# An attention, mixture-of-experts and feed-forward kernel: weights' fetches issued by another engine, one more stored table, smaller conditional blocks

## The chip, the cores and the metric

The kernel runs as one program on one core of a Trainium2 chip. The metric is the device time of one execution in microseconds (us), from the first to the last instruction and a little around them; lower is better. The engines are named as the profile names them: PE (matmul; PEld is its load of weights), DVE (vector), ACT (activation), POOL (GpSimd) and SP (which only issues transfers). A trailing q (ACTq, SPq) is an engine's sequencer: branches, register loads, semaphores and the issue of transfers.

## The reference

```python
def reference(**kw):                      # float32 but for moe2's weights (float64)
    a = exp(phi - max); a /= sum          # attention over 32 memory slots
    attn = softmax(q @ (a^T k)^T / 8) @ (a^T v)
    x = attn as (4608, 512)
    # top-1 mixture of 8 experts, FE = 1024
    e = argmax(cosine(x, emb) / tau); gate = softmax(...)[e]
    x = gate * (relu(x @ w1[e]) @ w2[e])
    # feed-forward, FF = 2048
    h = x @ w_in
    return (h * sigmoid(1.702 * h)) @ w_out
```

The tokens are 4608 rows of 512. Each matrix product is made of three f16 products of high and low parts, so that it has f32 accuracy.

## The kernel before

The span has four stretches. **Attention** takes the first 240 us. During it tokens are sorted by expert into a DRAM table `xbuf`. From about 240 to 304 us four **early slots** (s = -4 to -1) run for the tokens of one expert `e0` that are known early. Then come the **slots** s = 0 to 31: each takes 128 sorted tokens of one expert through both layers. From slot 28 (683 us) a slot also does halves of the **feed-forward**, which runs alone from about 800 us to the end.

One slot of the loop (`slot`, L1108) issues, in an order set by the table TIMES: the first layer of slot s (`product`, L981, 96 matmuls of 128x128), its ReLU in two halves (`relu`: ACT L994, DVE L997), the second layer of slot s - 1 (`second`, L1006, 24 matmuls of 128x512), the store of slot s - 2 (`leave`), the making of x16 and its transposing load xT for slot s + 2 (`take`: ACT L962, DVE L967, SP L969), the gather of slot s + 5 (`gather`, POOL L952), and shares of the decoding of the feed-forward's weights. These arrive as float64 (tiles `raw`, 512 KB each, SP L1252, three buffers, and three more that `Weights.widen` opens just ahead of slot 0) and are turned into f32 by ACT (L1278), DVE (L1281 to L1295) and POOL (L1299, L1304). A piece's POOL step frees its buffer and issues the next load.

An expert's weights are four pieces of w1 and four of w2 (tiles `wr`, 512 KB each) in one set of buffers. When a slot begins a new expert, conditional blocks run (`when`: an If on a register that SP, and the other engines, load from the table `tabs`, L834): `change(0, s + 1)` and `change(1, s)`. A change takes the scale, splits the f32 pieces `wr` into f16 pieces `wh` (ACT L80 writes the high part, DVE L91 the low part, piece by piece), and then `further` fetches the next expert's pieces into the same buffers (L842, on SP): a fetch has to wait for L91 of its piece. Two more blocks per slot, `bound(0)` and `bound(1)`, take squares of the fetched pieces on ACT (L846). All these Ifs stand in the code of L1120, and all five engines run each of them. `early` fetches the second expert's eight pieces in the early slots (`further(k, 0)`).

Completions of SP's transfers are counted by a ring of a few semaphores, and a transfer waits for the one that had its semaphore before. In the branch of a change that is not taken, SP has to wait for the four semaphores that the fetches would have used and count them on itself. So SP meets an earlier fetch that has not landed at its next change block.

`leave` (L1034) has POOL copy the tokens' indices into the last columns of the tile y16 (L1039), DVE write the scale next to them (L1040), ACT and DVE write the two f16 halves (L1043, L1046), and SP store the tile to `yb` (L1048) and the scale to `ys` (L1049). `Ffn.load` reads index and scale back from `yb`.

Of the kernel before, what the change touches and what calls it, by code (L numbers as in the profile page):

```python
# [27 lines left out]
XW = 514  # L28
YI, YS, YW = 2 * DM, 2 * DM + 2, 2 * DM + 4
HEAD = 8  # L30
EARLY = 4
ALWAYS = NT // P - EARLY
MORE = 6
ALONE = 28
LAG = 1
FIRST = 22.9, 5.4, 14.39, 33.37, 36.61, 2.87
# [612 lines left out]
class Dispatch:  # L649
# [43 lines left out]
    def slots(self):  # L693
# [5 lines left out]
        def up():  # L699
            o.ni = s.tile([P, E], I32, tag="ni", name="ni")  # L700
            v.tensor_scalar(o.ni, g.cnt, float(P - 1), None, ALU.add)
# [20 lines left out]
        def sum2():  # L722
            self.end = s.tile([P, E], F32, tag="end", name="end")
            v.tensor_reduce(out=self.end, in_=o.t8, axis=AX.X, op=ALU.add)
# [9 lines left out]
        def pick2():  # L734
            o.sl = s.tile([PB, ncols], F32, tag="sl", name="sl")
            v.tensor_reduce(out=o.sl, in_=o.t, axis=AX.X, op=ALU.add)
# [48 lines left out]


WHY = "counts of tokens, bounded by their number"

# [7 lines left out]
class Moe:  # L796
# [3 lines left out]
    def __init__(self, g, w):  # L800
        self.g = g

        shapes = [4, FE // 4], [2, DM]
        self.wh = [[w.tile([P, 2, *shapes[k]], F16, name=f"wh{k}{i}") for i in range(4)] for k in range(2)]
        self.raws = [[w.tile([P, *shapes[k]], F32, name=f"wr{k}{i}") for i in range(4)] for k in range(2)]
        self.sc = w.tile([P, 2], F32, name="scw")

        self.scp = w.tile([P, 1], F32, name="scp")
        g.junk = self.junk = w.tile([P, 1024], BF16, name="wjunk")
        self.m = w.tile([P, 2, 4], F32, name="wm")  # L810

# [5 lines left out]
        self.regs = {}  # L817

    def buf(self, kind):
        g = self.g  # L820
        if kind == "xg":
            return g.xp.tile([P, XW], F32, tag="xg", name="xg", bufs=3)
        if kind == "x16":
            return g.xp.tile([P, 2 * DM], F16, tag="x16", name="x16", bufs=2)
        if kind == "xT":
            return g.xp.tile([P, 8, P], F16, tag="xT", name="xT", bufs=2)
        if kind == "hT":
            return g.mp.tile([P, 2, 8, P], F16, tag="hT", name="hT")
        return g.mp.tile([P, YW], F16, tag="y16", name="y16")

    def reg(self, k, s):

        if (k, s) not in self.regs:
            self.regs[k, s] = self.g.nc.values_load(self.g.tabs[0:1, k, s:s + 1] if s >= 0 else self.g.before0[:, s + EARLY:s + EARLY + 1],  # L834
                                                    engines=(mybir.EngineType.SP,) if k in (0, 3, 4) else mybir.ALL_ENGINES,
                                                    min_val=0, max_val=(E - 1, 1, self.g.ns, 1, NT)[k],
                                                    skip_runtime_bounds_check_because=WHY)
        return self.regs[k, s]

    def fetch(self, k, i, ev):  # L840
        w = (self.g.w1, self.g.w2)[k][bass.ds(ev, 1)].rearrange("o (k p) f -> p (o k) f", p=P)
        self.g.nc.sync.dma_start(out=self.raws[k][i], in_=w[:, 2 * i:2 * i + 2] if k else w[:, :, FE // 4 * i:FE // 4 * (i + 1)])  # L842

# [36 lines left out]
    def first(self):  # L880
# [55 lines left out]
    def when(self, s):  # L936
# [3 lines left out]
        return self.g.tc.If(self.reg(1, s) > 0)  # L940

    def index(self, s):

# [10 lines left out]
    def take(self, s):  # L954
# [4 lines left out]
        def high():  # L959
            o.x16 = self.buf("x16")  # L960
            o.f = o.xg[:, DM + 1:DM + 2]
            nc.scalar.activation(out=o.x16[:, 0:DM], in_=o.xg[:, 0:DM], func=AF.Copy, scale=o.f)  # L962
            o.c = g.small.tile([P, 1], F32, tag="pc", name="pc", bufs=5)
            nc.scalar.activation(out=o.c, in_=o.xg[:, DM:DM + 1], func=AF.Copy)
# [43 lines left out]
    def measure(self, s):  # L1008
# [3 lines left out]
        def square():  # L1012
            o.m = g.small.tile([P, 1], F32, tag="ym", name="ym")
            nc.scalar.activation(out=self.junk[:, 0:DM], in_=o.yp, func=AF.Square, accum_out=o.m)  # L1014

            o.fac = g.small.tile([P, 1], F32, tag="fac", name="fac", bufs=4)
            nc.scalar.activation(out=o.fac, in_=o.c, func=AF.Copy, scale=self.scp)
# [14 lines left out]
    def leave(self, s):  # L1032
# [77 lines left out]
    def slot(self, s, share, ffn):  # L1110
# [16 lines left out]

        def bound(k):
            return lambda: self.bound(k)

        add(0, [lambda a=a, fi=fi: self.product(s, a, fi) for a in range(2) for fi in range(4)], h)
# [8 lines left out]
        if s:  # L1140
# [15 lines left out]
        if s + 5 < end:  # L1156
            add(TG, [lambda: self.gather(s + 5)])
        add(0.2, share, 10.2 / max(len(share), 1))
        for _, _, f in sorted(ev, key=lambda e: e[:2]):
            f()  # L1160

    def run(self, ffn):
# [11 lines left out]
        self.layer2(s)  # L1174
        with self.when(s):
            self.bound(0)
            self.bound(1)
        with self.when(s - 1):
            self.bound(1)

# [19 lines left out]
    def bounds(self, s):  # L1200
        with self.when(s):
            for k in range(2):
                self.bound(k)

# [192 lines left out]
class Ffn:  # L1397
# [16 lines left out]
    def load(self, t):  # L1414
# [8 lines left out]
        nc.sync.dma_start(out=o.s, in_=g.ys[rows].rearrange("(o r) w -> o (r w)", o=1).to_broadcast([P, 2 * P]))  # L1423
        o.i = g.small.tile([P, 2, YW - YI], F16, tag="x2i", name="x2i")
        nc.sync.dma_start(out=o.i, in_=g.yb[rows, YI:].rearrange("(j p) w -> p j w", p=P))
        o.f = g.small.tile([P, 2], F32, tag="x2f", name="x2f")
# [37 lines left out]
    def layer2(self, t, j):  # L1464
        g, nc, o = self.g, self.g.nc, self.x[t]
        if j == 0:
            nc.vector.tensor_scalar(o.f, o.i.bitcast(F32)[:, :, (YS - YI) // 2], self.k[:, 1:2], None, ALU.mult)
# [7 lines left out]
        nc.scalar.activation(out=y, in_=op, func=AF.Copy, scale=o.f[:, j:j + 1])  # L1475
        nc.gpsimd.indirect_dma_start(out=g.out, out_offset=bass.IndirectOffsetOnAxis(ap=o.i.bitcast(I32)[:, j, 0:1], axis=0), in_=y, in_offset=None,  # L1476
                                     bounds_check=NT - 1, oob_is_err=False)
# [40 lines left out]
def tile_kernel(ctx, tc, q, k, v, phi, emb, tau, w1, w2, w_in, w_out, out):  # L1518
# [11 lines left out]

    g.yb = dram.tile([NT + P, YW], F16, name="yb")
    g.ys = dram.tile([NT + P, 1], F32, name="ys")
# [12 lines left out]
    with tc.manual_schedule():  # L1545
# [17 lines left out]
        at.close()  # L1563
        g.weights.widen(wsr.enter_context(tc.tile_pool(name="wsr", bufs=1, side="right", reuse_waits="tile")))

# [38 lines left out]
```

## Time and profile before

| | us |
|---|---|
| median of 3 runs (1527.42 to 1529.71) | 1528.2 |
| profiled execution, its own time | 1527.33 |
| its span | 1525.6 |
| TensorE's mean granted clock | 0.956 of full speed |

The span runs from the first to the last instruction; the profiled execution's own time is 1.7 us more. Rows give a start and a duration in us of the span; in a timeline, the brackets hold the engine's idle time before a row and what ended it.

### The profile page before, as it was taken

The page shows a single profiled execution, that of the slowest core. Times are in us where ns is not written, and L with a number is a line of the kernel's source. Part 1 is how long each engine was busy: PE and PEld are TensorE (multiplying, and loading weights), DVE is VectorE, ACT ScalarE, POOL GpSimd, SP SyncE. Part 2 cuts the span into 40 slices and gives each one's busy share as a digit, 9 for nine tenths or more (in the row PEclk, how much of TensorE's full clock was granted, in tenths as well). Part 3 has the DMA queues.
Part 4 walks back from the last instruction along what each step waited for, and adds up shares of the span by engine and source line. Part 5 has one row for each costly group of instructions (what it writes and reads, how often), then busy time and mean ns, then how long its engine had stood idle before and what let it go on. Part 6 is the DMA issues. An engine that isn't in the chain of part 4 may idle for free. (4 is left out here: it accounts for less than half of the span.)

```text
span 1525.6 us, 31172 instructions
## 1 busy us (share of the span) xinstructions
PE 1379.8 (90%) x11628; PEld 972.9 (64%) x11628; DVE 839.3 (55%) x2066; ACT 691.9 (45%) x1623; POOL 274.6 (18%) x269
## 2 busy tenths in 40 slices
PE   5979888978789789889999999999989999999997
PEld 4767666656557566667657556666646666666664
DVE  3887896887557755856335144443324444443332
ACT  3767774445545554756334134333313333333332
POOL 2543430453323333210100000000000000000000
PEclk9997678989999999999999999999999999999999
DMA  9999933699987996673213411110211111101100
GB/s 221 239 240 266 233 73 110 179 170 162 159 109 121 172 117 83 163 93 39 56 47 32 60 32 40 31 31 19 34 32 27 32 27 30 32 19 28 32 15 14
DMA packets 171628, 138.11 MB, mean 91 GB/s; under 512 B 104730, under 2 KB 152218, under 8 KB 171426
## 3 DMA queue, kind: packets, MB, share of 16 engines
q1 hardware_dynamic: 165186, 115.13, 41.0%
q0 software_dynamic: 6240, 20.50, 5.5%
q8 instruction: 101, 1.65, 0.5%
q14 instruction: 101, 0.83, 0.4%
HBM read 84.77 MB, written 30.38 MB: 75 GB/s over the span
## 5 line engine op out<-in xcount | busy, mean ns | idle before, releaser
L1472 PE MATMUL op<-wo,gt 128*128 128x512 f16 x1728 | 378.9, 381 | 20.8 <-DVEq L1503 10.1
L1438 PE MATMUL hp<-x2T,wi 128*128 128x256 f16 x3456 | 380.7, 273 | 5.4 <-DMA x2T<-yb 2.9
L1438 PEld LDWEIGHTS <-wi 128*128 128x128 f16 x3456 | 337.8, 98 | 48.9 <-issue 3.6
L1442 DVE TENSOR_TENSOR th<-hp,x2s 128x256 f32<-128x256 f32 x288 | 122.1, 424 | 386.9 <-PE hp L1438 383.3
L1472 PEld LDWEIGHTS <-gt 128*128 128x128 f16 x1728 | 169.5, 98 | 224.7 <-issue 17.9
L981 PE MATMUL hp<-xT,wh 128*128 128x128 f16 x3552 | 216.7, 224 | 33.7 <-ACTq L1120 12.6
L981 PEld LDWEIGHTS <-wh 128*128 128x128 f16 x3552 | 210.1, 101 | 48.5 <-issue 30.2
L1006 PE MATMUL yp<-wh,hT 128*128 128x512 f16 x888 | 204.0, 387 | 22.7 <-ACT wjunk L846 5.2
L1443 ACT ACTIVATE th<-th,fk 128x256 f32<-128x256 f32 x288 | 146.2, 508 | 166.2 <-DVE th L1442 163.7
L1475 ACT ACTIVATE o<-op,x2f 128x512 f32<-128x512 f32 x36 | 24.7, 687 | 342.2 <-PE op L1472 342.2
L1006 PEld LDWEIGHTS <-hT 128*128 128x128 f16 x888 | 86.2, 99 | 127.8 <-PEq L1120 16.1
L1476 POOL DMA_INDIRECT out_dram<-o,x2i x36 | 35.2, 977 | 709.9 <-ACT o L1475 653.6
L1462 DVE SCALAR_TENSOR_TENSOR gt<-th,gt 128x256 f16<-128x256 f32 x288 | 120.4, 418 | 2.6
L1452 DVE SCALAR_TENSOR_TENSOR th<-th,hp 128x256 f32<-128x256 f32 x288 | 118.2, 410 | 3.1 <-ACT th L1443 3.1
L1454 ACT ACTIVATE gt<-th 128x256 f16<-128x256 f32 x288 | 115.6, 401 | 3.3 <-DVE th L1452 3.2
L952 POOL DMA_INDIRECT xg<-xbuf,idx x38 | 43.0, 1131 | 181.9 <-ACTq L1120 42.4
L997 DVE SCALAR_TENSOR_TENSOR hT<-hp,hT 128x512 f16<-128x512 f32 x74 | 50.6, 685 | 44.9 <-ACT hT L994 32.3
L367 PE MATMUL xp<-bdv,aT 128*96 128x264 f32 x192 | 68.8, 472 | 5.9 <-ACT aT L359 2.6
L994 ACT ACTIVATE hT<-hp 128x512 f16<-128x512 f32 x74 | 43.3, 587 | 57.2 <-PE hp L981 47.7
L846 ACT ACTIVATE wjunk<-wr 128x1024 bf16<-128x1024 f32 x48 | 50.6, 1054 | 22.2 <-SPq L1120 20.7
L1014 ACT ACTIVATE wjunk<-yp 128x512 bf16<-128x512 f32 x37 | 22.0, 595 | 79.7 <-PEq L1120 54.5
L1299 POOL TENSOR_TENSOR dlf<-dlf,raw 128x512 f32<-128x512 f32 x32 | 44.1, 1379 | 53.1 <-DVE raw L1295 45.6
(249 smaller groups left out, 1415.3 us busy)
## 6 DMA issues: line engine op xcount, KB each, us to landing
wr<-in_moe_w_dram SPq DMA_DIRECT2D x40, 512.0 KB, 10.2
xbuf<-xh SPq DMA_DIRECT2D x18, 576.0 KB, 9.8
yb<-y SPq DMA_DIRECT2D x37, 257.0 KB, 3.5
qr<-in_q_dram SPq DMA_DIRECT2D x16, 576.0 KB
kv<-in_k_dram SPq DMA_DIRECT2D x16, 576.0 KB, 7.9
kv<-in_v_dram SPq DMA_DIRECT2D x16, 576.0 KB
raw<-in_moe_w_in_dram SPq DMA_DIRECT2D x16, 512.0 KB, 8.4
raw<-in_moe_w_out_dram SPq DMA_DIRECT2D x16, 512.0 KB, 11.5
```

The lines of the kernel that those rows point to most:

```text
L367: nc.tensor.matmul(t[:PB], lhsT=self.aT[:, c], rhs=self.bdv, start=True, stop=True)
L846: self.g.nc.scalar.activation(out=self.junk, in_=flat(self.raws[k][i]), func=AF.Square, accum_out=self.m[:, k, i:i + 1])
L981: self.g.nc.tensor.matmul(o.hp[a][:, fi], lhsT=self.wh[0][f // 2][:, ta, k, f % 2 * P:f % 2 * P + P], rhs=o.xT[:, 4 * tb + k], start=(n == ...
L997: nc.vector.scalar_tensor_tensor(out=part(1), in0=o.hp[a], scalar=0.0, in1=part(0), op0=ALU.max, op1=ALU.subtract)
L1006: self.g.nc.tensor.matmul(o.yp, lhsT=o.hT[:, ta, k], rhs=self.wh[1][k // 2][:, tb, k % 2], start=(k + i == 0), stop=(k + i == 9))
L1438: nc.tensor.matmul(x.hp, lhsT=g.wi[:, ta, k, a * P:(a + 1) * P], rhs=o.xT[:, 4 * tb + k].rearrange("p j q -> p (j q)"), start=(i == 0), st ...
L1442: nc.vector.tensor_tensor(out=x.th, in0=x.hp, in1=o.s, op=ALU.mult)
L1443: nc.scalar.activation(out=x.th, in_=x.th, func=AF.Tanh, scale=self.k[:, 0:1])
L1452: nc.vector.scalar_tensor_tensor(out=x.th, in0=x.th, scalar=1.0, in1=x.hp, op0=ALU.add, op1=ALU.mult)
L1454: nc.scalar.activation(out=o.gt[-1][:, 0], in_=x.th, func=AF.Copy, scale=2.0**-GS)
L1462: self.g.nc.vector.scalar_tensor_tensor(out=o.gt[i][:, 1], in0=o.th[i], scalar=2.0**-GS, in1=o.gt[i][:, 0], op0=ALU.mult, op1=ALU.subtract)
L1472: nc.tensor.matmul(op, lhsT=o.gt[a][:, ta, j * P:(j + 1) * P], rhs=g.wo[:, a, tb], start=(i == 0), stop=(i == 47))
```

## The change

1. `fetch` takes an engine. The fetches of `further` go out from ACT's queue, those of `first` (during attention) stay with SP.
2. `reg` loads each register only on the engines listed for it in `ENGINES`: the expert's number and the flag for a further fetch (k = 0, 3) on ACT and SP, the flag of a change (k = 1) on all but POOL.
3. `bound`'s Ifs become `squares`, an If on ACT alone with a register load of its own.
4. `leave` has no index copy on POOL. The scale is in a tile of its own, y16 has 1024 columns instead of 1028, and a third store per slot, `yi`, writes the index straight from the table in SBUF. `Ffn.load` reads index and scale by two transfers instead of one.
5. `widen` is called in slot 1, 6 us into its table, instead of ahead of slot 0.
6. Some small tiles have fewer buffers.

```diff
+ENGINES = [[getattr(mybir.EngineType, n) for n in x.split()] for x in ("Activation SP", "Activation DVE PE SP", "Activation DVE PE Pool SP",
+                                                                       "Activation SP", "SP")]
...
-                                                    engines=(mybir.EngineType.SP,) if k in (0, 3, 4) else mybir.ALL_ENGINES,
+                                                    engines=ENGINES[k],
...
-    def fetch(self, k, i, ev):
+    def fetch(self, k, i, ev, e=None):
-        self.g.nc.sync.dma_start(out=self.raws[k][i], in_=w[:, 2 * i:2 * i + 2] if k else w[:, :, FE // 4 * i:FE // 4 * (i + 1)])
+        (e or self.g.nc.scalar).dma_start(out=self.raws[k][i], in_=w[:, 2 * i:2 * i + 2] if k else w[:, :, FE // 4 * i:FE // 4 * (i + 1)])
...
-                out.append((t + 0.4, lambda k=k, i=i: self.fetch(k, i, self.e0)))
+                out.append((t + 0.4, lambda k=k, i=i: self.fetch(k, i, self.e0, nc.sync)))
...
+    def squares(self, s, *ks):
+        if s not in self.runs:
+            self.runs[s] = self.g.nc.values_load(self.g.tabs[0:1, 1, s:s + 1], engines=(mybir.EngineType.Activation,), min_val=0, max_val=1,
+                                                 skip_runtime_bounds_check_because=WHY)
+        with self.g.tc.If(self.runs[s] > 0):
+            for k in ks:
+                self.bound(k)
...
-            o.s = o.y16[:, YS:YS + 2].bitcast(F32)
-            nc.gpsimd.tensor_copy(out=o.y16[:, YI:YI + 2].bitcast(I32), in_=self.index(s))
+            o.s = g.small.tile([P, 1], F32, tag="ysc", name="ysc", bufs=3)
...
+            nc.sync.dma_start(out=g.yi[r], in_=self.index(s))
...
-            add(TQ, [begins(s - 1, bound(0))] if s > 1 else [])
-            add(TQ1, [begins(s - 2, bound(1))] if s > 2 else [])
+            add(TQ, [lambda: self.squares(s - 1, 0)] if s > 1 else [])
+            add(TQ1, [lambda: self.squares(s - 2, 1)] if s > 2 else [])
...
+        if s == WIDE:
+            add(6, [self.widen])
...
-        nc.sync.dma_start(out=o.i, in_=g.yb[rows, YI:].rearrange("(j p) w -> p j w", p=P))
+        for x, y in ((o.i, g.yi), (o.w, g.ys)):
+            nc.sync.dma_start(out=x, in_=y[rows].rearrange("(j p) w -> p j w", p=P))
```

Three places show what stands on the queues. In the changed kernel line numbers are about 3 to 12 higher (L842 is L845 there, L994 is L1006, L916 is L919, L1120 is L1132). **The early fetches**: on SP before, the loads of the two registers, the If and the first fetches (an ISA row sets up the transfer in the row below it) stand behind the transposing load for an early slot:

```order
L969 DMA_TRANSPOSE xT<-x_3409 128x8x128
L834 TENSOR_LOAD tabs x2
L916 COMPARE_AND_BRANCH
L842 ISA
L842 DMA wr_134<-in_moe_w_dram 128x4x256
L842 ISA
L842 DMA wr_135<-in_moe_w_dram 128x4x256
```

On ACT now, the same stands between the two ReLU halves of one early slot (a row of ACT that ends in hT is a ReLU half):

```order
L1006 ACTIVATE hT<-hp 128x512
L837 TENSOR_LOAD tabs x2
L919 COMPARE_AND_BRANCH
L845 ISA
L845 DMA wr_135<-in_moe_w_dram 128x4x256
L845 ISA
L845 DMA wr_136<-in_moe_w_dram 128x4x256
```

Before, ACT's two ReLU halves stood side by side here; now eight fetches come between them.

**The change of w2's pieces**: on ACT before, four splits of wr (L80) and then the next block, the squares:

```order
L1120 COMPARE_AND_BRANCH
L80 ACTIVATE wh_130<-wr_138,wsv 128x1024
L80 ACTIVATE wh_131<-wr_139,wsv 128x1024
L80 ACTIVATE wh_132<-wr_140,wsv 128x1024
L80 ACTIVATE wh_133<-wr_141,wsv 128x1024
L916 UNCONDITIONAL_BRANCH
L1120 UNCONDITIONAL_BRANCH
L1120 COMPARE_AND_BRANCH
```

On ACT now, a second If and the four fetches stand behind the four splits (the first two are shown):

```order
L1132 COMPARE_AND_BRANCH
L80 ACTIVATE wh_131<-wr_139,wsv 128x1024
L80 ACTIVATE wh_132<-wr_140,wsv 128x1024
L80 ACTIVATE wh_133<-wr_141,wsv 128x1024
L80 ACTIVATE wh_134<-wr_142,wsv 128x1024
L919 COMPARE_AND_BRANCH
L845 ISA
L845 DMA wr_139<-in_moe_w_dram 128x2x512
L845 ISA
```

So ACT now does after its own splits what SP did before. **The same place on SP**: before, the four fetches stand behind the stores of y16:

```order
L834 TENSOR_LOAD tabs
L1048 ISA
L1048 DMA yb<-y_5224 128x1028
L1049 REGISTER_ALU
L1049 DMA ys<-y_5224 128x1
L1120 COMPARE_AND_BRANCH
L916 COMPARE_AND_BRANCH
L842 ISA
L842 DMA wr_138<-in_moe_w_dram 128x2x512
```

Now SP has the branches alone there, and the third store ahead of them:

```order
L837 TENSOR_LOAD tabs
L1059 ISA
L1059 DMA yb<-y_4758 128x1024
L1060 REGISTER_ALU
L1060 DMA ys<-ysc 128x1
L1061 REGISTER_ALU
L1061 DMA yi<-idx_68 128x1
L1132 COMPARE_AND_BRANCH
L919 COMPARE_AND_BRANCH
L919 UNCONDITIONAL_BRANCH x2
L1132 UNCONDITIONAL_BRANCH
```

The fetches have left SP's queue; the block itself, with its branches, has stayed.

## Rows read from the trace of the kernel before

**Rows 1.** Busy time by stage: the slots, and the feed-forward.
```profile
core 0: us, PE busy (x) PEld busy (x) DVE busy (x) ACT busy (x) POOL busy (x), PEclk, DMA share, GB/s
304.00:700.00 396.00, 337.99 (x3600) 243.64 (x3598) 273.07 (x533) 218.44 (x421) 125.06 (x122) 0.95 0.89 134
700.00:1526.00 826.00, 791.67 (x5565) 528.29 (x5562) 333.10 (x912) 285.95 (x661) 40.32 (x45) 0.99 0.15 31
```

**Rows 2.** PE's timeline in a slot of the loop without a change.
```profile
456.49 5.52 PE L981 MATMUL hp<-xT,wh 128*128 128x128 f16 x96
462.31 5.34 PE L1006 MATMUL yp<-wh,hT 128*128 128x512 f16 x24 [0.30 <-PEq L1120]
```

**Rows 3.** PE's timeline, the products that began late between 300 and 540 us.
```profile
318.21 6.99 PE L981 MATMUL hp<-xT,wh 128*128 128x128 f16 x80 [8.97 <-ACTq L1120]
...
391.87 2.72 PE L1006 MATMUL yp<-wh,hT 128*128 128x512 f16 x6 [5.24 <-ACT wjunk L846]
...
414.10 7.15 PE L981 MATMUL hp<-xT,wh 128*128 128x128 f16 x96 [4.12 <-DMA xT<-x]
...
517.15 7.39 PE L981 MATMUL hp<-xT,wh 128*128 128x128 f16 x96 [3.63 <-ACTq L1120]
...
536.78 7.82 PE L981 MATMUL hp<-xT,wh 128*128 128x128 f16 x96 [5.96 <-DMA xT<-x]
```

**Rows 4.** ACT's timeline ahead of the first of them.
```profile
315.93 0.66 ACT L1278 ACTIVATE dlf<-raw 128x512 f32<-128x512 uint32 x1 [6.95 <-SPq L1120]
```

**Rows 5.** SP's timeline around the change of w2's pieces in slot 5.
```profile
383.62 7.18 SPq L969 DMA_TRANSPOSE xT<-x  x1
393.02 2.32 SPq L842 DMA_DIRECT2D wr<-in_moe_w_dram  x4
...
410.98 1.28 SPq L969 DMA_TRANSPOSE xT<-x  x1
```

**Rows 6.** SP's timeline around the next change of w2's pieces, slot 14.
```profile
514.61 2.37 SPq L842 DMA_DIRECT2D wr<-in_moe_w_dram  x4
532.29 1.96 SPq L969 DMA_TRANSPOSE xT<-x  x1
```

**Rows 7.** What SP's queue waited for (us in total, times, longest).
```profile
SPq L1120 <- SPq L1120: 34.5, 24, 6.7
SPq L842 <- DVE wh L91: 19.3, 12, 7.0
```

**Rows 8.** ACT's timeline at these two changes.
```profile
382.93 4.27 ACT L80 ACTIVATE wh<-wr,wsv 128x1024 f16<-128x1024 f32 x4 [2.69 <-DVE wsv L876]
...
505.87 4.27 ACT L80 ACTIVATE wh<-wr,wsv 128x1024 f16<-128x1024 f32 x4 [3.59 <-DVE scw L923]
```

**Rows 9.** DVE's timeline at the second of them.
```profile
507.05 4.87 DVE L91 SCALAR_TENSOR_TENSOR wh<-wr,wsv,wh 128x1024 f16<-128x1024 f32 x4 [0.84 <-ACT wh L80]
```

**Rows 10.** SP's timeline at the early fetches.
```profile
281.75 9.89 SPq L842 DMA_DIRECT2D wr<-in_moe_w_dram  x8
```

**Rows 11.** ACT's timeline there.
```profile
277.97 0.60 ACT L994 ACTIVATE hT<-hp 128x512 f16<-128x512 f32 x1 [2.02 <-PE hp L981]
```

**Rows 12.** PE's timeline there.
```profile
288.31 5.78 PE L1006 MATMUL yp<-wh,hT 128*128 128x512 f16 x26
296.54 3.63 PE L1006 MATMUL yp<-wh,hT 128*128 128x512 f16 x16 [2.45 <-DVE hT L997]
```

**Rows 13.** The page: transfers of the experts' weights, median us to landing.
```profile
wr<-in_moe_w_dram SPq DMA_DIRECT2D x40, 512.0 KB, 10.2
```

**Rows 14.** Busy time around the product that began at 536.78, as group 1.
```profile
520.00:540.00 20.00, 13.10 (x126) 9.95 (x124) 10.10 (x19) 8.04 (x16) 6.52 (x6) 0.84 0.85 168
```

**Rows 15.** What POOL's copy of the index waited for.
```profile
POOL y L1039 <- DMA ys<-y: 107.6, 20, 15.1
```

**Rows 16.** Register loads and branches of the conditional blocks, ns min/median/max.
```profile
L834 ACTq TENSOR_LOAD <-tabs x38: 272/278/578, 316.1 to 1027.8; - x38
...
L1120 PEldq COMPARE_BRANCH  x129: 70/208/2077, 308.7 to 804.1; - x129
```

More of the change, by code (lines that the diff above doesn't have):

```diff
@@ L28 @@
 XW = 514
-YI, YS, YW = 2 * DM, 2 * DM + 2, 2 * DM + 4
 HEAD = 8
@@ L34 @@
 ALONE = 28
+WIDE = 1
 LAG = 1
@@ L699, in up @@
         def up():
-            o.ni = s.tile([P, E], I32, tag="ni", name="ni")
+            o.ni = s.tile([P, E], I32, tag="ni", name="ni", bufs=1)
             v.tensor_scalar(o.ni, g.cnt, float(P - 1), None, ALU.add)
@@ L722, in sum2 @@
         def sum2():
-            self.end = s.tile([P, E], F32, tag="end", name="end")
+            self.end = s.tile([P, E], F32, tag="end", name="end", bufs=1)
             v.tensor_reduce(out=self.end, in_=o.t8, axis=AX.X, op=ALU.add)
@@ L734, in pick2 @@
         def pick2():
-            o.sl = s.tile([PB, ncols], F32, tag="sl", name="sl")
+            o.sl = s.tile([PB, ncols], F32, tag="sl", name="sl", bufs=1)
             v.tensor_reduce(out=o.sl, in_=o.t, axis=AX.X, op=ALU.add)
@@ L816, in __init__ @@
         self.st = {}
-        self.regs = {}
+        self.regs, self.runs = {}, {}
     def buf(self, kind):
@@ L828, in buf @@
             return g.mp.tile([P, 2, 8, P], F16, tag="hT", name="hT")
-        return g.mp.tile([P, YW], F16, tag="y16", name="y16")
+        return g.mp.tile([P, 2 * DM], F16, tag="y16", name="y16")
     def reg(self, k, s):
@@ L962, in high @@
             nc.scalar.activation(out=o.x16[:, 0:DM], in_=o.xg[:, 0:DM], func=AF.Copy, scale=o.f)
-            o.c = g.small.tile([P, 1], F32, tag="pc", name="pc", bufs=5)
+            o.c = g.small.tile([P, 1], F32, tag="pc", name="pc", bufs=4)
             nc.scalar.activation(out=o.c, in_=o.xg[:, DM:DM + 1], func=AF.Copy)
@@ L1014, in square @@
             nc.scalar.activation(out=self.junk[:, 0:DM], in_=o.yp, func=AF.Square, accum_out=o.m)
-            o.fac = g.small.tile([P, 1], F32, tag="fac", name="fac", bufs=4)
+            o.fac = g.small.tile([P, 1], F32, tag="fac", name="fac", bufs=2)
             nc.scalar.activation(out=o.fac, in_=o.c, func=AF.Copy, scale=self.scp)
@@ L1174, in run @@
         self.layer2(s)
[L1175 to L1179, printed above, removed]
+        self.squares(s, 0, 1)
+        self.squares(s - 1, 1)
     def layer2(self, s):
@@ L1200, in bounds @@
     def bounds(self, s):
-        with self.when(s):
-            for k in range(2):
-                self.bound(k)
+        self.squares(s, 0, 1)
     def rest(self):
@@ L1423, in load @@
         nc.sync.dma_start(out=o.s, in_=g.ys[rows].rearrange("(o r) w -> o (r w)", o=1).to_broadcast([P, 2 * P]))
-        o.i = g.small.tile([P, 2, YW - YI], F16, tag="x2i", name="x2i")
-        nc.sync.dma_start(out=o.i, in_=g.yb[rows, YI:].rearrange("(j p) w -> p j w", p=P))
+        o.i = g.small.tile([P, 2, 1], I32, tag="x2i", name="x2i")
+        o.w = g.small.tile([P, 2, 1], F32, tag="x2w", name="x2w")
+        for x, y in ((o.i, g.yi), (o.w, g.ys)):
+            nc.sync.dma_start(out=x, in_=y[rows].rearrange("(j p) w -> p j w", p=P))
         o.f = g.small.tile([P, 2], F32, tag="x2f", name="x2f")
@@ L1466, in layer2 @@
         if j == 0:
-            nc.vector.tensor_scalar(o.f, o.i.bitcast(F32)[:, :, (YS - YI) // 2], self.k[:, 1:2], None, ALU.mult)
+            nc.vector.tensor_scalar(o.f, o.w[:, :, 0], self.k[:, 1:2], None, ALU.mult)
         op = g.psa.tile([P, DM], F32, tag="B", name="op", bufs=3)
@@ L1475, in layer2 @@
         nc.scalar.activation(out=y, in_=op, func=AF.Copy, scale=o.f[:, j:j + 1])
-        nc.gpsimd.indirect_dma_start(out=g.out, out_offset=bass.IndirectOffsetOnAxis(ap=o.i.bitcast(I32)[:, j, 0:1], axis=0), in_=y, in_offset=None,
+        nc.gpsimd.indirect_dma_start(out=g.out, out_offset=bass.IndirectOffsetOnAxis(ap=o.i[:, j], axis=0), in_=y, in_offset=None,
                                      bounds_check=NT - 1, oob_is_err=False)
@@ L1529, in tile_kernel @@
     g.xbuf0 = dram.tile([S + P, XW], F32, name="xbuf0")
-    g.yb = dram.tile([NT + P, YW], F16, name="yb")
+    g.yb = dram.tile([NT + P, 2 * DM], F16, name="yb")
+    g.yi = dram.tile([NT + P, 1], I32, name="yi")
     g.ys = dram.tile([NT + P, 1], F32, name="ys")
@@ L1563, in tile_kernel @@
         at.close()
-        g.weights.widen(wsr.enter_context(tc.tile_pool(name="wsr", bufs=1, side="right", reuse_waits="tile")))
+        wide = wsr.enter_context(tc.tile_pool(name="wsr", bufs=1, side="right", reuse_waits="tile"))
+        moe.widen = lambda: g.weights.widen(wide)
         def third():
```

2 lines of the change are left out of this document (removed).

## The prediction

> **What bounds the kernel now.** I read busy time by stage first [rows 1]. In the feed-forward PE works 791.67 of 826 us at a granted clock of 0.99 with a DMA share of 0.15; the change alters nothing there but one small load more per pair of token tiles, on a queue that is idle. In the slots (304 to 700 us) PE works 337.99 of 396 us, so 58 us lie there in gaps, with a DMA share of 0.89: that is the stage where the change can act. A slot without a change shows how little is lost when nothing is late [rows 2]: 5.52 us for the first layer's product, 5.34 us for the second's, and 0.30 us ahead of it for PE's own branch. The gaps sit at the slots that begin an expert. PE's timeline gives five between 300 and 540 us [rows 3]: 8.97, 5.24, 4.12, 3.63 and 5.96 us, together 27.9 us. The row after each says what ended the idle time: ACT's branch (8.97, 3.63), a transposed tile xT that landed late (4.12, 5.96), and once ACT's squares. Three of the first-layer products behind such gaps also run slowly, 7.15, 7.39 and 7.82 us against 5.52: the clock granted around the last of them is 0.84 [rows 14].
>
> The two gaps that end with xT are to be followed back along SP. The xT that PE waits for until 414.10 is issued at 410.98, and before it SP issued four wr fetches at 393.02 [rows 5]. The xT for 536.78 is issued at 532.29, and before it SP issued four wr fetches at 514.61 [rows 6]. A wr tile takes 10.2 us to land [rows 13], more when four share the engines. As the code has it, SP meets them again at the next change block, in the branch not taken, and stands until they land: SP's branches wait for SP's own transfers 24 times, 34.5 us in all, up to 6.7 us [rows 7]. So late wr fetches make late xT tiles.
>
> **The fetches go to ACT.** ACT has finished its four splits at 382.93 + 4.27 = 387.2 and at 505.87 + 4.27 = 510.1 us [rows 8]. A fetch also waits for DVE's low part, whose last ends at 507.05 + 4.87 = 511.9 [rows 9]. With four issues of 2.37 / 4 = 0.59 us each [rows 6], ACT issues at 510.2, 510.8, 511.4 and 512.0, and is through 2.3 us after its last split. SP in before began at 514.61 and at 393.02, since it had other things ahead in its order, among them a DMA_TRANSPOSE that held its queue for 7.18 us [rows 5]. So the w2 pieces start about 4.4 us earlier in slot 14 and 393.02 - 387.3 = 5.7 us earlier in slot 5. If they land that much earlier, SP reaches its xT that much earlier, and both gaps close to the 0.30 us of a quiet slot: gains of 3.8 and 5.7 us. (In slot 14 the product before is itself later by the next paragraph's 2.3 us, so 4.4 + 2.3 = 6.7 us cover the 5.96.) Where a gap closes the slow stretch behind it should go too: 7.15 - 5.52 = 1.6 and 7.82 - 5.52 = 2.3 us. Sum of gains: **13.4 us**; bounds 0 (the pieces land no earlier) and 13.4.
>
> The fetches of w1's pieces, and the third change, I cost at nothing: SP was not late there by rows that I can show, and no gap of theirs ends with xT. Bounds: a gain of as much as one gap more (4.1 us), and a loss of 2.3 us for each of three.
>
> **What ACT now waits for.** The 2.3 us are ACT's: behind the issue stand squares, a ReLU half, the next x16 and the branch that PE's next product waits for. In slot 14 that product waited 3.63 us for just this branch [rows 3], so there the delay goes to PE in full. I take it at all three changes that fetch w2: **+6.9 us**; bounds 0 (ACT catches up: it is busy 218 of 396 us [rows 1]) and 2.3 x 6 = 13.8 (the w1 changes too).
>
> **The early fetches.** SP needed 9.89 us from 281.75 to issue these eight, as the last four wait for transfers ahead of them [rows 10]. On ACT they stand ahead of the second ReLU half, which ran at 277.97 [rows 11] and would now come at 281.75 + 9.89 = 291.6. PE's second-layer product at 288.31 needs it from its middle on, 288.31 + 5.34 / 2 = 291.0, then the half itself (0.60 us) and DVE's low part: a stall of about 2 us, where ReLU halves queued behind delay the next one too. PE has a gap of 2.45 us at 294.09 anyway [rows 12], and 8.97 us at 309.23, of which an early loss can hide a part. I take **+1.5 us**; bounds 0 and 8 (the 9.9 us less the 2 us that PE has left).
>
> **Smaller parts.** Register loads: two or three more on ACT per slot, 278 ns each [rows 16], at most 0.9 us in a slot where ACT idles 45% of the time; hidden by that idle time, and if it is gone (in a change slot) 0.9 us more. Conditional blocks taken off PE, DVE, POOL and SP: PE's branch has a median of 208 ns [rows 16], but PE sits idle before the blocks that stay, not those that go; nothing, bounds 0 and a gain of 2.1 us (one branch at the longest, 2077 ns). The index copy: POOL waited 107.6 us for ys stores [rows 15], but POOL's later work (gathers five slots ahead, decoding for the feed-forward) is not what PE waits for in any row of group 3; nothing. In its place SP issues a third store, as long as its neighbours (0.59 us with its gap): nothing where no xT is due just behind it, at worst it delays that xT by 0.59 us. Later float64 buffers: the 8.97 us gap comes with ACT held 6.95 us at a raw tile [rows 4]. Fewer raw loads in flight in slot 0 may let xT and that tile land sooner, or starve the decoding and hold ACT again in slot 1; 0, bounds a gain of 8.7 (the gap gone) and a loss of 6.95 (one such hold more).
>
> **Sum.** -13.4 + 6.9 + 1.5 = -5.0 us against the profiled execution's own 1527.33: **1522.3 us**. That execution stands 0.9 us below the median of 1528.2, so a median of several runs could show up to 0.9 us more; I forecast 1522.5.
>
> The Trainium skill speaks against such a move: "DMA: Bandwidth & Descriptors", section "Issuing engines are not separate DMA queues", says that transfers started by different engines share the same 16 DMA engines and that starting them on several saves only the sequencer's time, usually small beside the transfer. By that rule the gain is sequencer time alone; the rows agree that it is SP's sequencer that was late, but put it at 4.4 and 5.7 us, not small. If it were small, the 13.4 us would be near 0 and the sum about 1536.
>
> **Rivals.** *Slower: ACT becomes the queue that holds PE.* Place: the early fetches and the six changes. A fetch blocks ACT until DVE's piece is done (SP's fetches waited for that 19.3 us in 12 waits, up to 7.0 [rows 7]) and until the transfer before it on its semaphore has landed. Price: 8 us early and 2.3 us at six changes, 13.8, with perhaps half of the gains kept, -6.7: +15, 1542; with the gains kept in full, 1536. It decides as soon as ACT leaves the early fetches later than 291 us and the next second-layer product shows a gap ended by a ReLU half. For it: the product at 517.15 already waited for ACT. Against it: ACT's load is 55%, and DVE's split trails ACT's by under 2 us.
>
> *Much faster: all change gaps shrink.* The 27.9 us of gaps and 5.8 us of slow products (1.6 + 1.9 + 2.3) are what there is between 300 and 540 us: two thirds of these 33.7 us gone would be -22, 1505. For it: SP is free between, so xT and the stores are never behind a fetch. Against: three of the five gaps are not SP's. The same page, section "Queues, rings and completion order", says that each DMA engine takes turns between the queues it has work for; then a transpose would no longer stand behind 2 MB of weights. No run here shows it yet.
>
> *No change: the DMA engines are the limit.* Their share is 0.89 through the slots [rows 1]. Four pieces issued earlier then land when they did, xT with them, and ACT's delay hides in the same gaps: 1527, give or take 3. Also here: the two effects cancel.
>
> **Chances and range.** Forecast case (1513 to 1524) 0.40; much faster 0.13; no change 0.20; slower 0.27. A measurement of this kernel tells a difference from none at about 0.2%, 3.1 us: faster means under 1525.1. Faster by more: 0.40 + 0.13 = 0.53; same 0.20; slower 0.27. The range goes from 1507 (most of the much faster case) to 1537 (the slower case with the gains kept); beyond are the worst early stall and the full gain. The forecast's own range is 1513 to 1525.
>
> **What would show it.** Right: wr issued from ACTq at about 510 to 512 and 387 to 390 us; the gaps before the products that began at 414.10 and 536.78 (4.12 and 5.96) at most 1 us, those products at 5.5 us; the 3.63 us gap grown to about 6; a new stall of about 2 us near 291. Wrong: an xT still issued over 10 us after the fetches with the same gap behind it (then landing, not issue, is the limit), ACT held over 10 us at the early fetches with PE idle for as long, or a gain that lies in the feed-forward, where I see none.

## The result, and the profile after

| us | before | after |
|---|---|---|
| median of 4 runs each | 1527.81 | 1547.39 |
| lowest and highest | 1524.85, 1529.71 | 1543.31, 1549.92 |
| ratio, 95% interval | | 1.0147 [1.0114, 1.0180] |

The change makes the kernel 1.5% slower. The forecast was 1522.5 us in a range of 1507 to 1537, so both the sign and the range were wrong. Executions over 1.5% above the fastest of the same kernel are left out of every ratio here and below; this matters mainly for e10, where 5 of 12 are left out.

Where it went is read first by stage. Busy time of the engines in the early slots, the slots and the feed-forward, after:

```profile
core 0: us, PE busy (x) PEld busy (x) DVE busy (x) ACT busy (x) POOL busy (x), PEclk, DMA share, GB/s
240.00:304.00 64.00, 50.43 (x556) 36.49 (x555) 44.67 (x139) 22.26 (x53) 12.80 (x8) 0.87 0.47 139
304.00:700.00 396.00, 332.23 (x3510) 232.59 (x3509) 258.04 (x505) 209.17 (x399) 115.75 (x92) 0.93 0.90 129
700.00:1526.00 826.00, 800.45 (x5658) 537.82 (x5657) 344.83 (x941) 293.59 (x680) 38.45 (x39) 0.99 0.15 33
```

In the slots PE gets 3510 matmuls done where it did 3600 [rows 1], at the same DMA share. Fixed windows mix a late start with a slow stage, so I cut the two traces by the work itself: a stage runs from the start of PE's first product of one slot to that of another, and the feed-forward from its own first product.

| stage, us | before | after | difference |
|---|---|---|---|
| attention, until slot -4 | 245.7 | 241.6 | -4.1 |
| early slots (-4 to -1) | 58.0 | 66.2 | +8.3 |
| slots 0 and 1 | 28.2 | 25.0 | -3.2 |
| slots 2 to 4 | 34.4 | 40.3 | +6.0 |
| slots 5 to 27 | 316.9 | 326.5 | +9.5 |
| feed-forward, to the end | 842.5 | 847.7 | +5.2 |

**The early slots.** ACT's timeline at the early fetches:

```profile
276.11 9.16 ACTq L845 DMA_DIRECT2D wr<-in_moe_w_dram  x8
285.46 0.60 ACT L1006 ACTIVATE hT<-hp 128x512 f16<-128x512 f32 x1 [15.13 <-DMA wr<-in_moe_w_dram]
```

DVE's timeline behind that:

```profile
290.48 3.65 DVE L1291 TENSOR_SCALAR wo<-wo 128x512 f32<-128x512 f32 x1
294.05 4.03 DVE L979 SCALAR_TENSOR_TENSOR x<-xg,x 128x512 f16<-128x512 f32 x1
298.01 0.68 DVE L1009 SCALAR_TENSOR_TENSOR hT<-hp,hT 128x512 f16<-128x512 f32 x1
```

And PE's:

```profile
286.12 3.49 PE L1018 MATMUL yp<-wh,hT 128*128 128x512 f16 x14 [0.95 <-ACT hT L1006]
298.74 6.11 PE L1018 MATMUL yp<-wh,hT 128*128 128x512 f16 x16 [9.14 <-DVE hT L1009]
```

Eight fetches keep ACT's queue for 9.16 us, as they kept SP's for 9.89 [rows 10]. On ACT a ReLU half stands behind them and idles 15.13 us. The first product that needs it loses only 0.95 us; the price falls one product later. DVE has fallen behind with it, and reaches the next half's low part (298.01) only after decoding and an x16: PE waits 9.14 us.

**Slots 2 to 4.** ACT's timeline, with two waits for a `raw` tile that was loaded late, and PE's behind the second:

```profile
317.62 0.66 ACT L1284 ACTIVATE dlf<-raw 128x512 f32<-128x512 uint32 x1 [6.45 <-DMA raw<-in_moe_w_in_dram]
...
338.99 0.67 ACT L1284 ACTIVATE dlf<-raw 128x512 f32<-128x512 uint32 x1 [5.48 <-DMA raw<-in_moe_w_in_dram]
```
```profile
345.82 5.52 PE L993 MATMUL hp<-xT,wh 128*128 128x128 f16 x96 [1.81 <-SPq L1132]
354.96 7.02 PE L1018 MATMUL yp<-wh,hT 128*128 128x512 f16 x24 [3.62 <-PEq L1132]
```

The hold that ACT had at 315.93 [rows 4] has not gone: it stands at 317.62, and a second one has come two slots later. Behind that PE has two gaps and a slow product that it did not have there.

**The two changes that the forecast was about.** ACT's timeline in slots 5 and 14:

```profile
391.63 4.27 ACT L80 ACTIVATE wh<-wr,wsv 128x1024 f16<-128x1024 f32 x4 [1.71 <-DVE wsv L879]
396.89 4.27 ACTq L845 DMA_DIRECT2D wr<-in_moe_w_dram  x4
401.44 1.06 ACT L1316 ACTIVATE wjunk<-wo 128x1024 bf16<-128x1024 f32 x1 [5.54 <-issue]
...
518.07 0.39 ACTq L845 DMA_DIRECT2D wr<-in_moe_w_dram  x1
518.60 1.13 ACT L80 ACTIVATE wh<-wr,wsv 128x1024 f16<-128x1024 f32 x1
523.13 4.33 ACTq L845 DMA_DIRECT2D wr<-in_moe_w_dram  x3
```

PE's timeline at both:

```profile
381.92 7.03 PE L1018 MATMUL yp<-wh,hT 128*128 128x512 f16 x24 [3.22 <-ACTq L1132]
...
408.44 7.72 PE L993 MATMUL hp<-xT,wh 128*128 128x128 f16 x96 [8.36 <-ACTq L1132]
...
506.11 8.24 PE L1018 MATMUL yp<-wh,hT 128*128 128x512 f16 x24 [4.34 <-DVE yr L1040]
...
524.45 7.61 PE L1018 MATMUL yp<-wh,hT 128*128 128x512 f16 x24 [4.60 <-DVE wo L1287]
...
535.54 7.38 PE L993 MATMUL hp<-xT,wh 128*128 128x128 f16 x96 [3.48 <-ACTq L1132]
```

No gap ends with xT here any more: that part of the forecast came true. But ACT is through 401.16 - 395.90 = 5.3 us after its last split in slot 5, and 527.46 - 519.73 = 7.7 us after it in slot 14. Where gaps ended with xT, others now end with ACT's branch or with DVE, and the products behind them are as slow as they were. The gaps have not shrunk: from the first product of slot 5 to that of slot 9, and from slot 14 to slot 18, PE's gaps over 1 us add up to 20.67 us in before and to 28.66 us here. The first stretch takes 61.1 us in before and 63.7 here, the second 60.2 and 70.0.

What the queues waited for (us in total, times, longest), after:

```profile
ACT hT L1006 <- DMA wr<-in_moe_w_dram: 15.1, 1, 15.1
```
```profile
SPq L1132 <- SPq L1132: 51.6, 29, 7.1
```

SP, which should have been freed, stands longer in its own branches than before: 51.6 us in 29 waits, against 34.5 in 24 [rows 7].

### The profile page after: what moved, and what is told of

It reads as the page before. It is cut to its first block, busy times and chain, and to the rows that moved or that the text cites. A ratio compares the mean times of both kernels' runs of the same rounds, so it can differ in the third digit from the quotient of the medians.

```text
span 1547.3 us, 30959 instructions
## 1 busy us (share of the span) xinstructions
PE 1383.2 (89%) x11628; PEld 964.0 (62%) x11628; DVE 833.0 (54%) x2066; ACT 692.0 (45%) x1623; POOL 262.3 (17%) x232
## 5 line engine op out<-in xcount | busy, mean ns | idle before, releaser
L1018 PE MATMUL yp<-wh,hT 128*128 128x512 f16 x888 | 215.0, 401 | 38.8 <-DVE hT L1009 9.1
L1006 ACT ACTIVATE hT<-hp 128x512 f16<-128x512 f32 x74 | 43.3, 587 | 58.7 <-PE hp L993 36.1
```

The source lines that it names most:

```text
L1018: self.g.nc.tensor.matmul(o.yp, lhsT=o.hT[:, ta, k], rhs=self.wh[1][k // 2][:, tb, k % 2], start=(k + i == 0), stop=(k + i == 9))
```

## The experiments

They ran in sets of up to four, each set on one chip beside the kernel before. On these chips before has medians of 1550 to 1560 us, so only ratios within a set are compared, and a stage is compared only with that of another experiment. A transfer that an experiment adds is read by nobody.

At first three theories stood: H, ACT is held by the fetches; S, the third store per slot costs more than its issue; W, the float64 buffers or the smaller blocks.

**Taking parts away from the change.** The first run puts all `further` fetches back on SP, the second only the early ones, the third takes the third store out (index and scale in y16 again). The fourth is the kernel before with the fetches on ACT.

```diff
 e1  self.fetch(k, i, e, self.g.nc.sync)
 e2  self.fetch(k, i, e, None if s else self.g.nc.sync)
 e3 -nc.sync.dma_start(out=g.yi[r], in_=self.index(s))
 e4 -self.g.nc.sync.dma_start(out=self.raws[k][i], ...)
 e4 +(e or self.g.nc.scalar).dma_start(out=self.raws[k][i], ...)
```

> The changed kernel with the further fetches issued by SP again (and their registers loaded on SP alone); all else as changed. Theory H (ACT is held by the fetches it issues, and PE behind it): the loss of 19.6 us goes, ratio to the kernel before 0.994 to 1.003, ACT's second ReLU half at the early fetches no longer waits. Rival S (the third store and its small packets, more waits of SP): stays at 1.010 or above. Rival W (float64 buffers opened later, smaller blocks): stays at 1.010 or above.

> The changed kernel with only the eight early fetches (slot 0's) issued by SP; the changes' fetches stay on ACT. Theory H, with the loss split as the two traces align (10.0 us in the early slots, 3.2 of it given back by slot 1; the rest at the three changes): 6 to 10 us better than the changed kernel, ratio to before 1.007 to 1.011. Rivals S and W: no difference from the changed kernel, 1.013 to 1.018.

> The changed kernel with index and scale in the tile y16 again (POOL's copy, two stores per slot, one load in the feed-forward); all else as changed. Theory H: still 1.010 to 1.018 of before. Rival S: 1.005 or below.

> The kernel before with one part of the change alone: the further fetches issued by ACT. Theory H: the whole loss, ratio 1.010 to 1.018. Rivals S and W: 0.998 to 1.004. My prediction's own working would give 0.996 to 0.998.

| run | ratio to before, 95% | early slots, us | slots 2 to 4, us |
|---|---|---|---|
| e1 all fetches on SP | 1.0149 [1.0102, 1.0196] | 58.7 | 45.6 |
| e2 early fetches on SP | 1.0184 [1.0128, 1.0240] | 60.4 | 46.5 |
| e3 no third store | 0.9980 [0.9946, 1.0013] | 68.9 | 42.8 |
| e4 before, fetches on ACT | 0.9990 [0.9954, 1.0025] | 68.1 | 33.8 |

H falls as the cause of the loss: with the fetches back on SP the change is as slow as it was, and ACT's fetches alone show neither a cost nor a gain (between a gain of 0.5% and a loss of 0.25%). The loss goes with the third store. That the queue makes no difference is what the Trainium skill says in "DMA: Bandwidth & Descriptors", section "Issuing engines are not separate DMA queues": transfers that several engines start share the same 16 DMA engines, and only the sequencer's time is saved. The runs agree, 0.9990.

The stages still show H and W, each in its place: the early slots take 68 to 69 us with the early fetches on ACT and 59 to 60 without, and slots 2 to 4 take 42.8 to 46.5 us with the later buffers and 34 without.

**Single parts put into the kernel before.** The store on its own, on POOL's queue, and with one element; the later buffers on their own; and, later, the smaller blocks and the early fetches on their own.

```diff
 e7  +nc.sync.dma_start(out=g.yi[r], in_=self.index(s))          # before, 128 rows x 4 B
 e8  +nc.sync.dma_start(out=g.yi[ds(reg, 1)], in_=...[0:1])       # before, one 4 B element
 e6  the change, with nc.gpsimd.dma_start(out=g.yi[r], ...)
 e9  before, with WIDE = 1
 e13 before, with squares(), ENGINES and the fewer buffers, all fetches on SP
 e17 before, with the fetches of further on ACT for s == 0 only
```

> The kernel before with a third store of 128 x 4 bytes per slot on SP's queue added (written, never read); nothing else. R and P both: 1.008 to 1.018. If it takes the parts together (third store and the rest of the change): below 1.005.

> As the run before, but the added store is a single 4-byte element, so one packet in place of 128. R (place in the ring, SP's issue time): within 0.004 of the run with 128 packets. P (packets): 0.997 to 1.004.

> The changed kernel with the third store (yi) issued by POOL, whose transfers are counted by semaphores of their own; the 128 packets of 4 bytes per slot stay. Theory R (the third store takes a place in SP's and ACT's ring of completion semaphores, so that the change blocks wait for other, later transfers): ratio to before 0.996 to 1.006. Rival P (the small packets themselves, or the DMA engines' time for them): 1.010 to 1.018, as with SP.

> The kernel before with the three further float64 buffers opened in slot 1 (6 us into it) in place of ahead of slot 0; nothing else. Theory W (the loss of 6.7 us that the traces show between 344 and 362 us in the three kernels with this part comes from it): 1.002 to 1.006. Otherwise 0.997 to 1.002.

> The kernel before with the smaller conditional blocks alone (squares in an If on ACT with its own register load, no change block on POOL, fetches on SP, no third store, buffers as before). My prediction's cost of nothing: 0.997 to 1.002. If the blocks taken off PE and SP matter: 0.985 to 0.996.

> The kernel before with the eight early fetches alone issued by ACT. By the four traces that have this part, the early slots grow by 9 to 11 us, of which slots 0 and 1 give 2 to 3 back: 1.003 to 1.006. My prediction's term for it was 1.5 us (1.001).

| run | ratio to before, 95% |
|---|---|
| e7 third store alone | 1.0134 [1.0090, 1.0178] |
| e8 the same with one element | 1.0028 [0.9996, 1.0059] |
| e6 change, third store on POOL's queue | 1.0455 [1.0417, 1.0494] |
| e9 buffers later, alone | 1.0032 [1.0009, 1.0055] |
| e13 smaller blocks alone | 0.9926 [0.9892, 0.9960] |
| e17 early fetches on ACT, alone | 1.0024 [0.9991, 1.0057] |

The store alone makes most of the loss. It is not its issue on SP: one element is issued as often and costs 0.6% at the most by its interval. Nor is SP the wrong queue for it: POOL's, where this line waits for the store before it, is far worse.

```profile
POOL yi L1061 <- DMA yi<-idx: 76.9, 12, 16.4
```

The later buffers alone bring PE's gap in slots 2 to 4 (41.2 us; PE's timeline of e9):

```profile
353.32 6.87 PE L1006 MATMUL yp<-wh,hT 128*128 128x512 f16 x24 [4.28 <-PEq L1120]
```

The early fetches alone bring theirs (67.7 us). ACT's and PE's timelines of e17 show the same picture as those of the change:

```profile
287.95 8.65 ACTq L842 DMA_DIRECT2D wr<-in_moe_w_dram  x8
296.80 0.60 ACT L994 ACTIVATE hT<-hp 128x512 f16<-128x512 f32 x1 [14.66 <-DMA wr<-in_moe_w_dram]
```
```profile
297.45 3.49 PE L1006 MATMUL yp<-wh,hT 128*128 128x512 f16 x14 [0.51 <-ACT hT L994]
310.08 2.31 PE L1006 MATMUL yp<-wh,hT 128*128 128x512 f16 x5 [9.14 <-DVE hT L997]
```

Yet the whole kernel loses only 0.24%, within its interval of none: slots 0 and 1 are shorter in e17 (25.2 us, where e9 and e13, with early fetches on SP, take 28.2 and 28.6), so part of the early loss is given back.

**What in the store costs?** Two theories: P, its 128 packets of 4 bytes load the DMA engines; R, it takes a turn in SP's ring of semaphores and lands late, so that what comes after waits. Stores of 16 and of 256 pieces of 4 bytes, one of 128 rows of 512 bytes, and a load of 128 x 4 bytes in the store's place:

```diff
 e10 +nc.sync.dma_start(out=g.yi[...16 rows...], in_=...[0:16])
 e11 +nc.sync.dma_start(out=g.yi[r]..., in_=o.y16[:, YI:YI + 4]...)   # 256 pieces of 4 B
 e15 +nc.sync.dma_start(out=g.yi[r], in_=o.y16[:, 0:256])
 e16 +nc.sync.dma_start(out=o.l, in_=g.w1[0, 0:P, 0:1])
```

> The kernel before with an added store per slot of 16 x 4 bytes on SP's queue (16 packets in place of the 128 that cost 1.3% and the one that cost 0.3%). The added store still lands only when all 16 DMA engines have come to it. Theory R2 (SP's change blocks wait for a late landing transfer; the landing counts, 11 us for 128 packets and 7 us for one): ratio 1.009 to 1.018. Theory P (the number of small packets counts): 1.000 to 1.006.

> The kernel before with an added store per slot of 256 pieces of 4 bytes on SP's queue (double the suspected cost). P: 1.020 to 1.030. R2: as with 128 packets, 1.009 to 1.018.

> The kernel before with a third store per slot of 128 packets of 512 bytes (the first quarter of y16, never read) on SP. If the number of packets counts: 1.010 to 1.018, as with 128 of 4 bytes. If it is their smallness (4 bytes written into a line): 0.998 to 1.006.

> The kernel before with a load per slot of 128 pieces of 4 bytes from DRAM into SBUF on SP (never used; one small tile has two buffers fewer to make room). If small writes into DRAM are what costs: 0.998 to 1.004. If small packets of either direction cost: 1.008 to 1.018.

| added per slot to the kernel before | ratio, 95% |
|---|---|
| e10 store of 16 x 4 B | 0.9997 [0.9953, 1.0041] |
| e7 store of 128 x 4 B | 1.0134 [1.0090, 1.0178] |
| e11 store of 256 x 4 B | 1.0197 [1.0137, 1.0257] |
| e15 store of 128 x 512 B | 1.0186 [1.0144, 1.0229] |
| e16 load of 128 x 4 B | 1.0114 [1.0074, 1.0155] |

The cost follows the number of pieces more than the bytes: 16 pieces cost 0.5% at the most, 128 of 4 bytes nearly as much as 128 of 512, and a load about as much as a store. (The medians of all executions in e10's set, 1561.39 and 1553.64, differ by 0.5% as well.) It is not a fixed price per piece: P looked for 2 to 3% with 256 pieces, and their interval overlaps that of 128. R has a hard time: by the semaphores' updates in its trace the store of 16 pieces lands as late as `ys` beside it, 10.7 and 11.1 us in the median, holds its turn as long, and costs little. SP's waits in its own branches, 34.5 us in before [rows 7], are 43.4 us in e10 and 49.0 in e7, so most of their growth comes with the cheap store too.

**The same rule used on the kernel before.** If 128 pieces cost that much, then the store that before always had, `ys`, should cost something too. A transpose on DVE puts the 128 scales into four rows of 128 bytes:

```diff
-nc.sync.dma_start(out=g.ys[r], in_=o.s)
+nc.vector.tensor_copy(out=self.sq[:, 0:1], in_=o.s)
+nc.vector.transpose(out=st, in_=self.sq)
+nc.sync.dma_start(out=g.ys[r].rearrange("(a b) w -> a (b w)", b=32),
+                  in_=st.rearrange("(a b) w -> a b w", b=32)[:, 0])
```

e19 is before with this alone. e12 is the change without the third store, with the buffers early and the early fetches on SP; e14 is e12 with this store; e18 is the change with `yi` stored this way and `ys` as it was.

> The changed kernel without the third store, with the float64 buffers opened ahead of slot 0 again, and with the early fetches on SP; the fetches of the changes stay on ACT, squares in an If on ACT alone. If the losses are the third store (1.3%), the buffers (0.3%) and the early fetches on ACT: 0.990 to 1.000, a version at least as fast as both kernels. If ACT's fetches at the changes cost too: 1.000 to 1.008.

> The version of the last set that beat both (no third store, early fetches on SP, float64 buffers opened early, smaller blocks; 0.991) with the scale's store too made small: DVE turns the 128 scales round (two short instructions more per slot), and ys is stored as 4 packets of 128 bytes in place of 128 of 4 bytes. Theory P (each store of 128 small packets costs about 1.3%, whichever it is): 0.975 to 0.985. If the scale's store costs nothing, or DVE's two instructions eat it: 0.988 to 0.996.

> The changed kernel with all its parts; only the third store is made small: DVE turns the 128 indices round (two short instructions per slot) and yi is stored as 4 packets of 128 bytes in place of 128 of 4 bytes. If the number of packets is what made the change slower: as the changed kernel without the third store, 0.994 to 1.003. If the third store costs by its place in SP's order or its semaphore: 1.008 to 1.018.

> The kernel before with the scale's store alone made small in the same way (a few small tiles have fewer buffers to make room, as in the change). If the store of 128 packets costs what its removal gave on top of the other parts (1.8%): 0.978 to 0.988. If it needed the other parts: 0.990 to 0.998.

| run | ratio to before, 95% | median, us |
|---|---|---|
| e12 rest of the change | 0.9909 [0.9870, 0.9947] | 1537.92 |
| e14 e12, `ys` in four rows | 0.9731 [0.9696, 0.9766] | 1505.17 |
| e18 change, `yi` in four rows | 1.0167 [1.0110, 1.0225] | 1571.42 |
| **e19 before, `ys` in four rows** | **0.9644 [0.9597, 0.9691]** | **1494.19** |

e19 beats both kernels, by 56 us against the 1550.25 of before in its set. Busy time in its slots, to be held against [rows 1]:

```profile
304.00:700.00 396.00, 362.55 (x3827) 257.80 (x3825) 291.37 (x634) 235.89 (x456) 126.53 (x123) 0.98 0.50 135
```

The DMA share falls from 0.89 to 0.50 while the same is moved (134 and 135 GB/s). The share goes with `ys`: e14, with four rows as well, has 0.50 too, while e18, in e19's set, still has `ys` in 128 pieces and 0.90:

```profile
304.00:700.00 396.00, 321.52 (x3298) 224.87 (x3297) 250.28 (x540) 199.11 (x382) 115.95 (x92) 0.90 0.90 127
```

By queue in the same window (packets, MB, share of 16 engines), before and then e19:

```profile
q1 hardware_dynamic: 58735, 44.26, 77.0%
```
```profile
q1 hardware_dynamic: 55022, 44.38, 40.9%
```

Some 3,700 of this queue's 58,735 packets have gone, 124 for each of 30 stores, and with them nearly half of the time of the others. In a view of 35 us this is plain to see. The DMA engines from 440 to 475 us (busy tenths, and GB/s), before and then e19:

```profile
DMA  9990814245412004991917779995395999994700
GB/s 157 202 56 0 61 14 28 9 52 197 139 33 17 0 0 92 61 263 14 89 61 249 108 47 80 103 51 28 37 77 74 229 231 310 376 419 19 19 0 0
```
```profile
DMA  0000787734790000087799710000000003988779
GB/s 0 9 0 9 150 150 193 294 125 37 183 370 28 0 0 0 0 167 133 187 412 291 297 33 0 0 0 0 0 0 0 9 0 57 343 279 233 256 261 266
```

Before, slices that are nine tenths busy often move only 51 to 103 GB/s; in e19 a slice that is seven tenths busy or more moves 133 to 412, and the engines rest in between. Between issue and the last update of its semaphore, a `wr` piece took 11.2 us in the median of the slots and takes 5.1, an xT 8.0 and 3.2, a `raw` tile 10.4 and 4.3. SP's wait in its own branches shrinks with that, from 34.5 us in 24 waits [rows 7]:

```profile
SPq L1125 <- SPq L1125: 13.4, 19, 2.2
```

The Trainium skill's page "DMA: Bandwidth & Descriptors" has both halves of the advice. "Rules for kernel authors" says to merge many small transfers into one large one; e19 keeps the number of transfers and merges the pieces of one, which is near that advice but not a test of it. "Specifications" wants at least 512 B per transfer for full rate; rows of 512 B in e15 cost as much as pieces of 4 B, so here the number of pieces told more than their size.

Turning the only store of single elements gives 3.6%, more than P looked for (0.978 to 0.988), and adding a second one costs 1.3% (e7). The DMA share agrees that the first one weighs more: it is 0.50 in the slots of the two kernels without such a store, 0.88 to 0.99 in those with one, and not higher with two on SP's queue (0.90 to 0.96). One thing more goes with e19's edit: `ys` no longer reads y16, so POOL's copy of the index does not wait for it (107.6 us before [rows 15]). This was not tried apart; in the changed kernel that copy and its wait are gone too, and it gains nothing.

What stays open: why some 6% of the queue's packets hold up the rest is not shown. And e18 stores `yi` in 4 packets and still loses 1.67%, where the change without `yi` loses nothing and before bears a store of 16 pieces for 0.5% at the most. So inside the change it is not the packets alone. SP's waits in its own branches do not explain it (46.6 us, where e10 has 43.4). Its DVE copy and transpose, its place ahead of the next xT and its turns in SP's ring were not tried apart.

## Why the prediction was wrong

- **The third store, taken as nothing: this is the step that failed.** It was priced as an issue on SP, 0.59 us, hidden unless an xT stands behind it. SP's own rows confirm the issue as short (0.33 us in the median of `yi`); but e7 measures the store alone at 1.34%, about 21 us per execution, and without it the change loses nothing (e3). By e7 against e8 the price goes with the pieces that the store is cut into, and not with the issue; e18 says that inside the change this is not all of it. The share of 0.89 [rows 1] was on the table, and POOL's 107.6 us of waits for `ys` [rows 15] too; the prediction read the first as a lot of traffic and the second as harmless. The first was the mark of the 128-piece store that the change doubles: 134 GB/s moved at a share of 0.89 where 0.50 does. The second said that the 512 bytes of `ys` land late, as late as 512 KB of weights (10.9 us in the profile's median, and 10.2 [rows 13]).
- **The gains, 13.4 us: right on the first wait, wrong on the gap.** xT no longer ends a gap there. But a gap was to close to 0.30 us with the wait that ended it, and other waits stood close behind, ACT's branch and DVE: PE's gaps around the two changes grew from 20.67 to 28.66 us, where 9.5 were to go, and the products behind them stayed slow (7.03 to 8.24 us). How much of that the third store makes is not shown. In e4, with the fetches alone on ACT, two gaps in the same slots still end with xT (2.04 and 4.21 us), so the fetches on SP were not all that made it late.
- **ACT's delay at a change, 2.3 us each:** 5.3 and 7.7 us. The prediction counted four issues. In slot 5 they took 4.27 us rather than 2.37, and in slot 14 three of them began only 3.4 us after the last split: a fetch waits there for more than DVE's piece, the last of which was done at 521.52. The trace shows for what: the semaphores of these three fetches got their last updates at 522.98, 523.56 and 526.93 us, from the transfers that had them before, a `ys` and a `yi` store issued at 512.46 and 513.02 and a `raw` tile issued at 515.47. So the late landing of the small stores holds ACT too. For the whole kernel e4 gives 0.9990 [0.9954, 1.0025]. This is near the rival "no change", but it does not exclude the -5.0 us of the forecast (0.9967). Whether the DMA engines are the reason, as that rival had it, is not shown: in e14, where their share is 0.50, the moved fetches do not help either.
- **The early fetches, +1.5 us (0 to 8):** +8.3 us in the early slots and -3.2 in the next two; alone +0.24% or 3.7 us (e17). Within the bounds. The stall was looked for at the first product (0.95 us came) and stood at the second (9.14), through DVE's queue. One sign of being wrong that the prediction named came true here: ACT held over 10 us (15.13), with PE idle for nearly as long.
- **Later float64 buffers, 0 (-8.7 to +6.95):** +0.32%, 5 us, in slots 2 to 4 (e9). The bound "one such hold more" is what came; the middle was not.
- **Smaller blocks, 0 (0 to a gain of 2.1 us):** a gain of 0.74%, about 11 us (e13). The prediction looked for PE's wait at its own branches. Which engine's blocks give the gain was not tried apart.
- **The feed-forward, where none was seen:** 5.2 us longer in the profiled execution; no run separates the two small loads per pair from the rest, and kernels without them differ as much (from the start of slot 28 on, e9 takes 846.8 us and e17 856.3).

The rival with the right sign, "ACT becomes the queue that holds PE", gave 1536 to 1542, but for the wrong reason: it holds in the early slots, and not over the whole kernel. The rival "much faster" did not come either: xT, on a queue without the experts' weights, took 10.0 us to land (median of the slots) where it took 8.0 in before; with `ys` in four rows it takes 3.1 us in e14, the weights on ACT's queue, and 3.2 in e19, the weights on SP's. The single parts add up to +1.34 (store) + 0.32 (buffers) - 0.10 (all fetches on ACT) - 0.74 (blocks) = +0.8%, with some 0.7% either way from their intervals together; measured are 1.47%. The two agree within that, though not closely, and e18 says that the store costs more inside the change than beside the old kernel.

## What to carry to other kernels

Price a transfer by the pieces that it is cut into, not only by its bytes or by the time that its issue takes: one more transfer of 128 pieces per slot cost this kernel 1.1 to 1.9% (e7, e15, e16), and turning the one that it always had into four rows gave 3.6%. When the DMA share is near 0.9 and the GB/s are low in the same slices, look for the transfer with one element per partition, and turn it (a transpose on an idle engine) before moving queues about. Moving fetches to another queue paid nothing here, and on an engine that computes, whatever stands behind the fetch waits with it.

## What was not expected of the hardware

- With a store of 128 elements of 4 bytes about once in 14 us (28 in 396 us), the DMA engines stood at a share of 0.89, where it was 0.50 with four rows of 128 bytes, and the other transfers took about twice as long (`wr` 11.2 us against 5.1). The small packets themselves have records of 9 ns in the median; the time shows in the records of the others, and there in a few long ones: the packets of 4096 bytes have a median of 159 ns in both kernels, but a mean of 460 ns in before and 205 in e19, and the longest takes 8.5 us and 1.5.
- A store of 16 such elements cost 0.5% at the most; 128 rows of 512 bytes cost as much as 256 elements of 4.
- With that store on POOL's queue the change cost 4.55% instead of 1.5%.
- With the DMA share at 0.50 the moved fetches and smaller blocks do not help any more: e14, which has both, stands at 0.9731, e19, which has neither, at 0.9644. Which of the two takes the gain back was not tried.
